# Banded attention with global tokens and a squared-ReLU MLP on one core: global value products in other slots, output copies at the top of a slot, global softmax behind the activation, weight decoding later

## The chip, the cores and the metric

The kernel runs on one core of one Trainium2 chip. The metric is the device time of one execution in microseconds (us), lower is better. Durations come from one profiled execution, the times from unprofiled runs.

## What is computed

Eight batches of eight heads, 512 local tokens, 32 global tokens, head size 64. A local query sees the keys within 32 positions and all global keys; a global query sees every key. The result, 4608 rows of 512, goes through an MLP with 2048 hidden units, squared ReLU, no bias. Everything is float32.

```python
k_all = np.concatenate([k_g, k_l], axis=2); v_all = np.concatenate([v_g, v_l], axis=2)
out_g = np.matmul(sm(scale * np.matmul(q_g, k_all.transpose(0, 1, 3, 2))), v_all)
s_ll = np.where(np.abs(pos[:, None] - pos[None, :]) <= 32, scale * np.matmul(q_l, k_l.transpose(0, 1, 3, 2)), -1e9)
s_lg = scale * np.matmul(q_l, k_g.transpose(0, 1, 3, 2))
out_l = np.matmul(sm(np.concatenate([s_lg, s_ll], axis=-1)), np.concatenate([v_g, v_l], axis=2))
x = np.concatenate([out_g, out_l], axis=2).transpose(0, 2, 1, 3).reshape(B * S, H * D)
h = np.maximum(x @ w_in, 0.0)
out = h * h @ w_out
```

Here `sm` is the softmax over the last axis.

## The kernel before

The local work is cut into 128 units t: eight heads for each half (256 queries) of each batch. Eight units make 256 rows of x, which are one MLP block; 16 local blocks and one block of all 256 global rows make 17. A block takes eight MLP steps, each with 256 of the 2048 hidden units.

One loop over slots t = 0 to 145 writes the whole program. Slot t does, for attention, the transposes of unit t-1's probabilities (`transposes`, copied out by `pt_evac` into pts), the scores and softmax of unit t+1 (`begin`, `rise`; ACT takes the exponential, `softmax3` the division a slot later), and in odd slots the value products of the pair t-3, t-2 into one PSUM tile, xa (`av`); `x_evac` then splits xa into a rounded part x_h (ACT) and the rest x_l (DVE). For the MLP it does step m = t-9: `gemm1` (x times w_in into h), `act1` (ReLU on ACT into r, the square r on DVE), `gemm2` of step m-1 (into the two tiles of o), `act2` (the split of r into gh on ACT and gl on DVE). Products of split operands take three matmuls. Blocks start where m % 8 is 0, slots 17, 25, 33 and so on. At m % 8 == 1 `evac` copies the finished block's o into ot on ACT and sends it out; the new block's first `gemm2` writes the same o.

The 32 global rows run along: each unit's scores hold its global queries' scores too, collected in sg (`g_copy`, `g_add`). After every four units of a batch's second half, so twice in 16 slots, a chain of jobs follows, put on a list by slot and place: `g_soft` (DVE maximum), `g_exp` (ACT exponential), `g_norm` (two small DVE steps), `g_load_v` (gv), `g_tr` (transposes), `g_evac` (copies into gp), `g_av` (ten value products, in the other half of xa), `g_xs` (ACT, xa into gxs) and `g_x` (eight 32x32 DVE transposes into xg). For the second batch these lists start at units 27 and 31, and so on every 16 slots.

The weights come as 64-bit numbers in 32 chunks: a load (`w_load`, into wr), a conversion on ACT (`w_abs`, into wf) and two DVE steps (`w_bits`, the letter "b" in the table `PLAN`). From block 1 on split weights are used: `w_split` (letter "s") makes ws, one ACT and one DVE step. `PLAN` has a row for each slot from 0 and four places in it: behind the softmax, ahead of `act1`, behind `act2` and at the end. `w_need` does ahead of its place what a step needs at once. `LOOK` is how many chunks ahead of the decoding loads are issued, as far as buffers are free (32 in all). Units below 16 use unsplit float32 operands, as does block 0.

TensorE's instructions keep the written order throughout; VectorE's and ScalarE's from slot 17 on (`FREE`), before that a scheduler orders them. All loads and stores are on one queue, SP's. On each engine an instruction that waits holds those behind it. All compute instructions are recorded by one helper, line 53, so the profile is read by tile names.

Of the kernel before, what the change touches and what calls it, by code (L numbers as in the profile page):

```python
# [7 lines left out]
F32 = mybir.dt.float32  # L8
# [8 lines left out]
P = 128  # L17
# [8 lines left out]
NSTEP = NBLK * 8  # L26
# [2 lines left out]
SCALE = 0.125  # L29
CHUNKS = ((0, 128), (320, 128), (128, 96), (224, 96))  # L30

PLAN = [",,,b", "b,,,b", "b,,,b", "b,,b,", "b,,b,", "b,,b,", "b,,b,", "b,b,,b", "b,b,,b", "bb,bb,bb,bb", "bb,bb,bb,bb", "bbs,bb,bbs,bbs", "bbs,bbs,bbs,bbs", "bbs,bbs,bbs,bbs", "bbs,bbs,bs,s", "ss,s,s,s", "ss,s,s,s", "s,,s,", "s,,s,", "s,,s,", "s,,s,", "s,,s,", "s,,s,"]
FREE = (17, 17, 0)
LOOK = 2
SQ = (0, 8)
WCH = 32

# [1 line left out]
def f(ap):  # L39
    return ap.bitcast(F32)  # L40
# [19 lines left out]
def attention_moe(  # L60
# [10 lines left out]
    nc = tc.nc  # L71
# [4 lines left out]
    p2 = ctx.enter_context(tc.tile_pool(name="p2", bufs=2))  # L76
# [15 lines left out]
    def w_take(n):  # L92
        w_bufs["free"] -= n

    def load_head(t):
        raw = pq.tile([P, QK], F32, tag="raw", name=f"raw{t}")
        v = pv.tile([P, VC], F32, tag="v", name=f"v{t}")
        nc.sync.dma_start(raw, qk[t])
        nc.sync.dma_start(v, vv[t])
        heads[t] = dict(raw=raw, v=v)  # L100

    load_head(0)
    con = cp.tile([P, P + 4 * WIN], F32, name="con")
    for o, e in ((0, P + 2 * WIN), (P + 2 * WIN, P + 4 * WIN)):
        nc.sync.dma_start(con[:, o:e], consts[:, o:e])
# [154 lines left out]
    def x_evac(t):  # L260
        g, c = t // 8, (t % 8) // 2
        x = xa[:, :HALF]
        if g == 0:
            ac.copy(xg[:, c, :], x)
        else:
            ac.copy(x_h[:, g % 2, c, :], x)
            ve.tensor_sub(x_l[:, g % 2, c, :], x, f(x_h[:, g % 2, c, :]))
        heads[t] = heads[t + 1] = None

    state = {}  # L270

    def g_load(t):

        b, grp = t // 16, (t // 4) % 2
        qr = p2.tile([P, P], F32, tag="qr", name=f"qr{t}")
        nc.sync.dma_start(qr, qg[b, grp])
        state["q", t // 4] = qr

    def g_split(t):
        if plain(t):  # L280
# [144 lines left out]
    def act2(m):  # L425
        r = moe["r"]
        if m < 8:
            moe["g", m] = (r,)
            return
        gh = p2.tile([P, 2, HALF], F32R, tag="gh", name=f"gh{m}")  # L430
        gl = p2.tile([P, 2, HALF], F32R, tag="gl", name=f"gl{m}")
        ac.copy(gh, r)
        ve.tensor_sub(gl, r, f(gh))
        moe["g", m] = (gh, gl)
# [23 lines left out]
    def evac(blk, tiles=(0, 1)):  # L458
        for i in tiles:
            ot = p2.tile([P, DM], F32, tag="ot", name=f"ot{blk}_{i}")  # L460
            ac.copy(ot, moe["o"][i])
            if blk < NGR:
                b, hf = divmod(blk, 2)
                r0 = b * 544 + 32 + hf * 256 + i * P
                nc.sync.dma_start(out[r0 : r0 + P, :], ot)
            else:
                for bb in range(4):
                    r0 = (4 * i + bb) * 544
                    nc.sync.dma_start(out[r0 : r0 + 32, :], ot[32 * bb : 32 * bb + 32, :])
# [4 lines left out]
    def w_start(i):  # L474
        while w_next["load"] < min(WCH, i + LOOK) and w_bufs["free"] >= 2:
            w_take(1)
            w_load(w_next["load"])
            w_next["load"] += 1
        if i < w_next["load"] and i not in w_ready and (i % 2 == 1 or w_bufs["free"] >= 1):
            w_ready.add(i)  # L480
            w_abs(i)
# [29 lines left out]
    def w_tick(t, place):  # L511
        if t < len(PLAN):
            for c in PLAN[t].split(",")[place]:
                {"b": w_pass, "s": w_chunk}[c]()
# [19 lines left out]
    def run_jobs(t, place):  # L534
        for job, *args in jobs.pop((t, place), ()):
            job(*args)

    def begin(t):
        scores(t)
        g_scores(t)  # L540

    def rise(t):
        softmax1(t)
        softmax2(t)

    g_load(0)
    w_start(0)
    begin(0)
    rise(0)
# [2 lines left out]
    for t in range(NSTEP + LAG + 1):  # L552
        m = t - LAG
        ve.on, ac.on, pe.on = [t >= x for x in FREE]
        prev, run, live, more = 1 <= t <= NT, 0 <= m < NSTEP, t < NT, t + 1 < NT
        pair = t - 3 if t % 2 and 3 <= t <= NT + 1 else None
        if t + 4 < NT:
            load_head(t + 4)
        if t % 4 == 0 and t + 4 < NT:
            g_load(t + 4)  # L560
        if run:
            w_need(m)

        if pair is not None:
            av(pair)
            x_evac(pair)
        run_jobs(t, "av")
        run_jobs(t, "tr")
        if prev:
            transposes(t - 1)  # L570
        if more:
            begin(t + 1)
        if run:
            gemm1(m, 0)
            gemm1(m, 1)
        if prev:
            pt_evac(t - 1)
        run_jobs(t, "evac")
        if live:
            softmax3(t)  # L580
        if t + 2 < NT:
            split_head(t + 2)
        if more:
            rise(t + 1)
        if 0 < m <= NSTEP and m % 8 == 1 and m > 8:
            evac(m // 8 - 1)
        w_tick(t, 0)
        if more:
            g_copy(t + 1)
            g_add(t + 1)  # L590
        run_jobs(t, "soft")
        if t % 4 == 2 and t + 2 < NT:
            g_split(t + 2)
        w_tick(t, 1)
        if run:
            act1(m)
        run_jobs(t, "late")
        if live and t % 4 == 3 and (t // 8) % 2 == 1:
            d = t if t % 8 == 3 else t + 1
            e = d + 4 if d % 2 else d + 5  # L600
            for at, place, job in (
                (d + 1, "soft", g_soft),
                (d + 1, "soft", g_exp),
                (d + 2, "soft", g_norm),
                (d + 2, "late", g_load_v),
                (d + 3, "tr", g_tr),
                (d + 3, "evac", g_evac),
                (e, "av", g_av),
                (e, "evac", g_xs),
                (max(e, 17), "late", g_x),  # L610
            ):
                jobs.setdefault((at, place), []).append((job, t))
        if m == NSTEP:
            for i in range(2):
                gemm2(m - 1, 0, (i,))
                gemm2(m - 1, 1, (i,))
                evac(NBLK - 1, (i,))
        elif m > 0:
            gemm2(m - 1, 0)
            gemm2(m - 1, 1)  # L620
        if run:
            act2(m)
        w_tick(t, 2)
        if 0 < m <= 8:
            w_done(m - 1)
        w_tick(t, 3)
        if 8 * NGR - 2 <= m < 8 * NGR:
            cols = (slice(0, 224), slice(224, HALF))[m % 2]
            ac.copy(x_h[:, 0, :, cols], xg[:, :, cols])
            ve.tensor_sub(x_l[:, 0, :, cols], xg[:, :, cols], f(x_h[:, 0, :, cols]))  # L630
# [69 lines left out]
```

## Time and profile before

| | |
|---|---|
| median of 3 runs | 1136.09 us (1134.98 to 1137.07) |
| profiled execution | 1137.75 us, its span 1135.9 |
| PE, DVE, ACT busy in the span | 1052.2, 669.6, 552.6 us |
| mean granted clock | 0.972 |
| HBM read, written | 65.54 MB, 8.91 MB |

A row of the timeline has the start, the time until the end, engine, line, operation, tiles written and read, shape and count; in square brackets the engine's idle time before it and who ended that. A row of the waits has the total, the number and the longest. A row by stretch has its limits, its length, then busy time of PE, PEld, DVE, ACT and POOL with instruction counts, the granted clock, the share of the DMA engines that is busy and GB/s. Matmuls overlap, so their durations don't add up; start to start does.

### The profile page before, as it was taken

The numbers are of one execution on the slowest core, as the hardware profiler recorded it, in microseconds if no ns is written. First come the engines' busy times: TensorE is split into PE (matmuls) and PEld (weight loads), VectorE is DVE, ScalarE is ACT, GpSimd is POOL, SyncE is SP. The second block draws the span as 40 slices with busy tenths as digits, with TensorE's granted clock in tenths as the row PEclk, the third lists the DMA queues.
The fourth block names the chain that finished last, engine by engine and source line by source line (L and its number), as shares of the span: only waits on it lengthen the run. The fifth ranks groups of instructions, "written<-read, shape, count | busy, mean of one in ns | idle before, by whom it ended". The sixth has DMA issues, their size and how long they took to land.

```text
span 1135.9 us, 21870 instructions
## 1 busy us (share of the span) xinstructions
PE 1052.2 (93%) x8320; PEld 878.9 (77%) x8320; DVE 669.6 (59%) x2340; ACT 552.6 (49%) x1617; POOL 0.5 (0%) x5
## 2 busy tenths in 40 slices
PE   5898799998999989998999989998999989999998
PEld 4665578877888778877888778877888778878987
DVE  5886466565666556655666656656566666663321
ACT  5786445545554445544455454545454454543222
POOL 0000000000000000000000000000000000000000
PEclk9798989999999999999999999999999999999999
DMA  8881111121211212121211212112211212101000
GB/s 267 275 298 52 32 58 48 52 62 57 61 56 40 62 53 62 59 59 48 66 42 53 62 52 62 58 53 61 57 45 56 58 53 66 43 1 43 1 20 19
DMA packets 72458, 75.88 MB, mean 67 GB/s; under 512 B 6304, under 2 KB 63776, under 8 KB 72352
## 3 DMA queue, kind: packets, MB, share of 16 engines
q1 hardware_dynamic: 72352, 74.47, 21.6%
q8 instruction: 66, 1.08, 0.4%
q14 instruction: 40, 0.33, 0.1%
HBM read 65.54 MB, written 8.91 MB: 66 GB/s over the span
## 4 chain that ended last, share of the span: by engine, by line
PE 53%; DVE 23%; ACT 14%; issue 4%; DMA 4%; SPq 0%; ACTq 0%; DVEq 0%
PE o L53 22%; PE h L53 19%; PE xa L53 6%; DVE prob L53 6%; ACT prob L53 5%; PE sb L53 3%; DVE gl L53 3%; DVE r L53 3%; ACT gh L53 2%; PE pt L53 2%; DVE st L53 2%; DVE lo L53 2%; ACT r L53 2%; ACT sg L53 2%; DMA wr<-in_w_dram 2%
## 5 line engine op out<-in xcount | busy, mean ns | idle before, releaser
L53 PE MATMUL h<-x_h,ws 128*128 128x256 f32 x2048 | 400.8, 289 | 6.1 <-DVE r L53 6.1
L53 PE MATMUL o<-ws,gh 128*128 128x512 f32 x1024 | 326.2, 400 | 25.7 <-ACT ot L53 25.7
L53 PEld LDWEIGHTS h<-x_h,ws 128*128 128x128 f32 x2048 | 327.6, 191 | 22.0 <-DVE r L53 7.5
L53 PE MATMUL h<-x_l,ws 128*128 128x256 f32 x1024 | 289.9, 283 | 0.1
L53 ACT ACTIVATE prob<-prob,st 128x224 f32<-128x224 f32 x256 | 121.3, 475 | 259.9 <-DVE st L53 259.7
L53 PEld LDWEIGHTS o<-ws,gh 128*128 128x128 f32 x1024 | 187.0, 192 | 62.2 <-ACT ot L53 29.3
L53 PE MATMUL o<-ws,gl 128*128 128x512 f32 x512 | 203.5, 398 | 0.0
L53 PEld LDWEIGHTS h<-x_l,ws 128*128 128x128 f32 x1024 | 196.1, 192 | 1.0 <-DVE x_l L53 0.4
L53 DVE TENSOR_TENSOR sg<-sb,sg 32x128 f32<-32x128 f32 (+3 forms) x280 | 60.1, 257 | 159.5 <-ACT sg L53 159.3
L53 DVE TENSOR_TENSOR r<-h,r 128x512 f32<-128x512 f32 x128 | 88.4, 691 | 104.2 <-ACT r L53 104.0
L53 DVE TENSOR_TENSOR gl<-r,gh 128x512 fp32r<-128x512 f32 x128 | 88.7, 693 | 77.3 <-ACT gh L53 76.8
L53 ACT CAST gh<-r 128x512 fp32r<-128x512 f32 x128 | 79.3, 619 | 97.5 <-DVE r L53 97.5
L53 PEld LDWEIGHTS o<-ws,gl 128*128 128x128 f32 x512 | 97.7, 191 | 22.9
L53 ACT ACTIVATE r<-h 128x512 f32<-128x512 f32 x136 | 81.3, 598 | 61.1 <-PE h L53 58.1
L53 DVE CUSTOM_DVE_ANT_0 prob<-sb,con 128x224 f32<-128x224 f32 x248 | 86.4, 386 | 9.4 <-PE sb L53 9.1
L53 DVE COPY pts<-pt 128x256 f32<-128x256 f32 x128 | 53.5, 418 | 40.5 <-PE pt L53 40.0
L53 DVE TENSOR_SCALAR prob<-prob,st 128x224 f32<-128x224 f32 x256 | 74.7, 334 | 4.2
L53 ACT COPY pts<-pt 128x256 f32<-128x256 f32 x128 | 47.5, 371 | 60.0 <-PE pt L53 59.0
L53 PEld LDWEIGHTS xa<-pts,v 128*64 128x64 f32 (+1 forms) x768 | 47.5, 141 | 35.8 <-issue 24.1
L53 PEld LDWEIGHTS pt<-con,prob 64*128 64x128 f32 (+1 forms) x1024 | 42.3, 137 | 41.5 <-issue 27.5
L53 PE MATMUL xa<-pts,v 128*64 128x128 f32 (+1 forms) x768 | 73.9, 327 | 0.2 <-ACT pts L53 0.2
L53 PE MATMUL pt<-con,prob 64*128 64x64 f32 (+1 forms) x1024 | 61.7, 242 | 8.0 <-DVE prob L53 7.9
(69 smaller groups left out, 1050.4 us busy)
## 6 DMA issues: line engine op xcount, KB each, us to landing
raw<-in_qk_dram SPq DMA_DIRECT2D x128, 176.0 KB, 2.3
wr<-in_w_dram SPq DMA_DIRECT2D x32, 512.0 KB, 5.5
v<-in_vv_dram SPq DMA_DIRECT2D x128, 96.0 KB, 1.9
gv<-in_vg_dram SPq DMA_DIRECT2D x32, 320.0 KB, 3.4
out_dram<-ot SPq DMA_DIRECT2D x32, 256.0 KB, 2.0
qr<-in_qg_dram SPq DMA_DIRECT2D x32, 64.0 KB, 2.3
out_dram<-ot SPq DMA_DIRECT2D x8, 64.0 KB, 1.7
con<-in_consts_dram SPq DMA_DIRECT2D x1, 288.0 KB, 4.3
```

The source lines that it names most:

```text
L53: r = method(*args, **kwargs)
```

## The change

Five things move; the instructions are the same ones, in the same numbers, on every engine.

- `evac` goes from behind `rise` to the top of the slot, ahead of everything that ACT does in it.
- `g_av` and `g_xs` go from odd slots (where `av` runs) to even ones: one slot later for one of the two chains, one earlier for the other.
- `g_soft`, `g_exp`, `g_norm` and `g_x` go to a new place, "post", behind `act2`; they were ahead of `act1`, `g_x` between `act1` and `act2`.
- `PLAN` does fewer decode steps in slots 0 to 8 and fewer splits before slot 17; `LOOK` goes from 2 to 4.
- the first global queries (qr of `g_load(0)`) are loaded behind unit 0's inputs, not behind the masks and units 1 to 3.

```diff
-PLAN = [",,,b", "b,,,b", "b,,,b", "b,,b,", "b,,b,", "b,,b,", "b,,b,", "b,b,,b", "b,b,,b", "bb,bb,bb,bb", ...]
+PLAN = [",,,b", ",,,b", ",,,b", ",,,b", ",,,b", ",,,b", ",,,b", ",,,b", "b,b,b,b", "b,bb,bbb,bb", ...]
-LOOK = 2
+LOOK = 4
...
     load_head(0)
+    g_load(0)
...
-    g_load(0)
     w_start(0)
...
+        if m > 8 and m % 8 == 1:
+            evac(m // 8 - 1)
         if pair is not None:
             av(pair)
             x_evac(pair)
...
-        if 0 < m <= NSTEP and m % 8 == 1 and m > 8:
-            evac(m // 8 - 1)
         w_tick(t, 0)
...
-            e = d + 4 if d % 2 else d + 5
+            e = d + 5 if d % 2 else d + 4
             for at, place, job in (
-                (d + 1, "soft", g_soft),
-                (d + 1, "soft", g_exp),
-                (d + 2, "soft", g_norm),
+                (d + 1, "post", g_soft),
+                (d + 1, "post", g_exp),
+                (d + 2, "post", g_norm),
                 (d + 2, "late", g_load_v),
                 (d + 3, "tr", g_tr),
                 (d + 3, "evac", g_evac),
                 (e, "av", g_av),
                 (e, "evac", g_xs),
-                (max(e, 17), "late", g_x),
+                (max(e, 17), "post", g_x),
...
             act2(m)
+        run_jobs(t, "post")
         w_tick(t, 2)
```

ScalarE around slots 33 and 34, first before, then changed (gst31: the global exponential; r24, gh24: step 24; ot2: block 2's output; pts33, hi36: unit 33's transposed probabilities, unit 36's rounded inputs):

```order
L53 ACTIVATE sg_107,gst31_2864<-sg_107,gst31_2864 128x544
L53 ACTIVATE r24_2868<-h24_2818 128x512
L53 CAST gh24_2883<-r24_2868 128x512
L53 COPY pts33_2934<-pt0_112 128x4x64
L53 CAST hi36_2941<-raw36_2699 128x352
L53 ACTIVATE prob1_109,st35_2945<-prob1_109,st35_2945 128x224 x2
L53 COPY ot2_0_2951<-o0_2_2165 128x512
L53 COPY ot2_1_2954<-o1_2_2166 128x512
```

```order
L53 ACTIVATE r24_2864<-h24_2818 128x512
L53 CAST gh24_2879<-r24_2864 128x512
L53 ACTIVATE sg_109,gst31_2883<-sg_109,gst31_2883 128x544
L53 COPY ot2_0_2891<-o0_2_2165 128x512
L53 COPY ot2_1_2894<-o1_2_2166 128x512
L53 COPY pts33_2940<-pt0_114 128x4x64
L53 CAST hi36_2947<-raw36_2679 128x352
L53 ACTIVATE prob1_111,st35_2951<-prob1_111,st35_2951 128x224 x2
```

The global exponential has moved from ahead of r24 to behind gh24, and the two output copies from behind the softmax exponentials to right behind it, ahead of pts33 and hi36.

TensorE at the global value products of the chain of unit 27, before (slot 31) and changed (slot 32):

```order
L53 MATMUL xa_114<-pts29_2534,v29_1987 64x128
L53 MATMUL xa_114<-pts28_2430,v28_1896 64x128
L53 MATMUL xa_114<-pts29_2534,v29_1987 64x128
L53 MATMUL xa_114<-gv27_2458,gp27_2537 64x128 x10
L53 MATMUL pt0_112<-con_89,prob0_108 128x64
```

```order
L53 MATMUL o0_2_2165<-ws23_1477,gl21_2581 128x512
L53 MATMUL o1_2_2166<-ws23_1477,gh21_2580 128x512 x2
L53 MATMUL o1_2_2166<-ws23_1477,gl21_2581 128x512
L53 MATMUL xa_116<-gv27_2456,gp27_2537 64x128 x10
L53 MATMUL pt0_114<-con_91,prob1_111 128x64
```

They stood behind the pair 28, 29's local value products in the same tile; now they stand behind a w_out product, in a slot without local ones.

VectorE at `g_x` of the same chain, before (slot 31) and changed (slots 32 and 33):

```order
L53 TENSOR_TENSOR r22_2672<-h22_2624,r22_2672 128x512
L53 STREAM_TRANSPOSE xg_106<-gxs27_2652 32x32 x8
L53 TENSOR_TENSOR gl22_2696<-r22_2672,gh22_2695 128x512
L53 COPY pts31_2748<-pt1_113 128x4x64
L53 TENSOR_SCALAR st32_2662<-st32_2662 128x2
```

```order
L53 TENSOR_TENSOR r23_2761<-h23_2713,r23_2761 128x512
L53 TENSOR_TENSOR gl23_2777<-r23_2761,gh23_2776 128x512
L53 STREAM_TRANSPOSE xg_108<-gxs27_2741 32x32 x8
L53 TENSOR_TENSOR x_l_107<-xa_116,x_h_106 128x256
L53 COPY pts32_2843<-pt1_115 128x4x64
```

The eight transposes have moved from between r and gl to behind gl, ahead of the next slot's x_l.

More of the change, by code (lines that the diff above doesn't have):

```diff
@@ L30 @@
 CHUNKS = ((0, 128), (320, 128), (128, 96), (224, 96))
-PLAN = [",,,b", "b,,,b", "b,,,b", "b,,b,", "b,,b,", "b,,b,", "b,,b,", "b,b,,b", "b,b,,b", "bb,bb,bb,bb", "bb,bb,bb,bb", "bbs,bb,bbs,bbs", "bbs,bbs,bbs,bbs", "bbs,bbs,bbs,bbs", "bbs,bbs,bs,s", "ss,s,s,s", "ss,s,s,s", "s,,s,", "s,,s,", "s,,s,", "s,,s,", "s,,s,", "s,,s,"]
+PLAN = [",,,b", ",,,b", ",,,b", ",,,b", ",,,b", ",,,b", ",,,b", ",,,b", "b,b,b,b", "b,bb,bbb,bb", "b,bb,bbb,bb", "b,bb,bbbs,bbs", "b,bb,bbbs,bbs", "bs,bb,bbbs,bbs", "bs,bb,bbbs,bbs", "b,bb,bbss,bs", "s,s,s,", "s,,s,s", "s,,s,s", "s,,s,", "s,,s,", "s,,s,", "s,,s,", "s,,s,"]
 FREE = (17, 17, 0)
-LOOK = 2
+LOOK = 4
 SQ = (0, 8)
@@ L100, in load_head, with g_load @@
         heads[t] = dict(raw=raw, v=v)
+    state = {}
+    def g_load(t):
+        b, grp = t // 16, (t // 4) % 2
+        qr = p2.tile([P, P], F32, tag="qr", name=f"qr{t}")
+        nc.sync.dma_start(qr, qg[b, grp])
+        state["q", t // 4] = qr
     load_head(0)
+    g_load(0)
     con = cp.tile([P, P + 4 * WIN], F32, name="con")
@@ L268, in x_evac @@
         heads[t] = heads[t + 1] = None
[L270 to L277, printed above, removed]
     def g_split(t):
```

## The prediction, made before the changed kernel ran

> **What bounds the kernel now.** I read the page's first part, then PE's waits, the busy time by stretch, and the rows of one repeated piece in order of time.
>
> ```profile
> span 1135.9 us, 21870 instructions
> PE 1052.2 (93%) x8320; PEld 878.9 (77%) x8320; DVE 669.6 (59%) x2340; ACT 552.6 (49%) x1617; POOL 0.5 (0%) x5
> ...
> PE xa L53 <- DVE x_l L53: 28.6, 15, 5.4
> PE o L53 <- ACT ot L53: 25.7, 15, 3.8
> ...
> PE h L53 <- DVE r L53: 6.1, 7, 1.1
> PE sb L53 <- DMA qr<-in_qg_dram: 4.6, 1, 4.6
> ```
>
> PE is busy in 93% of the span, so of the 1135.9 us only 84 are idle. PE's own waits name 60.4 of them: 28.6 in which the global value products (into xa) wait for DVE's x_l, 25.7 in which a block's first w_out product (into o) waits for ACT's output copies ot, and 6.1 in which a w_in product (into h) waits for DVE's square r. The 4.6 for qr comes once, at the start.
>
> From slot 26 on the program repeats every 16 slots. The busy time of early stretches, of six such pieces together, of one of them, and of 3.4 us around one wait; then PE's rows from the one piece:
>
> ```profile
> 28.40:56.80 28.40, 23.68 (x150) 17.74 (x151) 23.53 (x88) 20.24 (x65) 0.00 (x0) 0.76 0.82 275
> 88.80:106.36 17.56, 12.12 (x77) 8.57 (x75) 13.69 (x34) 12.32 (x32) 0.00 (x0) 0.81 0.10 26
> 106.36:114.37 8.01, 8.01 (x44) 5.29 (x42) 2.94 (x13) 3.63 (x10) 0.00 (x0) 1.00 0.37 107
> 123.39:204.12 80.73, 72.50 (x562) 59.27 (x561) 49.80 (x174) 39.07 (x114) 0.00 (x0) 0.92 0.17 50
> 204.12:980.80 776.68, 732.49 (x6123) 621.22 (x6121) 476.99 (x1730) 383.24 (x1165) 0.00 (x0) 0.98 0.19 56
> 333.11:462.00 128.89, 121.51 (x1023) 103.14 (x1021) 79.50 (x289) 63.87 (x195) 0.00 (x0) 0.99 0.20 56
> 372.70:376.10 3.40, 3.04 (x30) 2.71 (x32) 0.31 (x1) 0.00 (x0) 0.00 (x0) 0.50 0.02 5
> ...
> 373.06 2.40 PE L53 MATMUL xa<-gv,gp 128*64 128x128 f32 x20 [2.28 <-DVE x_l L53]
> 424.06 1.31 PE L53 MATMUL xa<-gv,gp 128*64 128x128 f32 x20 [0.95 <-DVE x_l L53]
> 438.78 1.09 PE L53 MATMUL xa<-pts,v 96*64 96x256 f32 x12
> 453.31 1.09 PE L53 MATMUL xa<-pts,v 96*64 96x256 f32 x12
> ...
> 398.79 0.39 PE L53 MATMUL h<-x_h,ws 128*128 128x256 f32 x1 [0.84 <-DVE r L53]
> 404.19 0.73 PE L53 MATMUL o<-ws,gh 128*128 128x512 f32 x2 [2.28 <-ACT ot L53]
> ```
>
> Six pieces take 776.68, one 129.4 on the mean; in the one of 128.89 DVE is busy for 79.5 and ACT for 63.9. Such a piece has PE waits of 2.28 and 0.95 (xa), of 2.28 and, in another slot, about 1.0 (ot), and of 0.84 (r): 7.4. In the 3.4 us at a 2.28 us wait the granted clock is 0.50, which costs 1.7 more; over six pieces it is 0.98, so 2% or some 14 us, eight such windows. What PE needs without waits: a slot with and a slot without local value products take 14.53 together (438.78 to 453.31), eight pairs 116.2; with two global value products at 1.31 and two sets of global transposes at about 0.36 (an estimate: eight matmuls of 64 columns) it is 119.6.
>
> **The second limit is the round of ACT and DVE.** Both run in written order from slot 17 on, and a slot's work goes to and fro between them. Rows of slots 48 to 53, where a tile's name tells the step:
>
> ```profile
> 386.49 0.48 ACT L53 ACTIVATE prob<-prob,st 128x224 f32<-128x224 f32 x1 [2.81 <-DVE st L53]
> 390.03 0.69 DVE L53 TENSOR_TENSOR gl<-r,gh 128x512 fp32r<-128x512 f32 x1 [0.69 <-ACT gh L53]
> 390.76 0.42 DVE L53 TENSOR_TENSOR x_l<-xa,x_h 128x256 fp32r<-128x256 f32 x1
> 393.71 0.48 ACT L53 ACTIVATE prob<-prob,st 128x224 f32<-128x224 f32 x1 [2.25 <-DVE st L53]
> 395.60 0.72 DVE L53 TENSOR_REDUCE gst<-sg 128x1 f32<-128x544 f32 x1
> 396.55 0.75 ACT L53 ACTIVATE sg<-sg,gst 128x544 f32<-128x544 f32 x1 [1.33 <-DVE gst L53]
> 397.41 0.60 ACT L53 ACTIVATE r<-h 128x512 f32<-128x512 f32 x1
> 399.30 0.36 ACT L53 COPY pts<-pt 128x256 f32<-128x256 f32 x1
> 399.42 0.69 DVE L53 TENSOR_TENSOR gl<-r,gh 128x512 fp32r<-128x512 f32 x1 [0.69 <-ACT gh L53]
> 399.56 0.49 ACT L53 CAST hi<-raw 128x352 fp32r<-128x352 f32 x1
> 400.03 0.42 DVE L53 COPY pts<-pt 128x256 f32<-128x256 f32 x1
> 401.26 0.52 DVE L53 TENSOR_TENSOR lo<-raw,hi 128x352 fp32r<-128x352 f32 x1
> 402.64 0.48 ACT L53 ACTIVATE prob<-prob,st 128x224 f32<-128x224 f32 x1 [2.59 <-DVE st L53]
> 403.58 1.05 ACT L53 COPY ot<-o 128x512 f32<-128x512 f32 x2
> 409.42 0.41 DVE L53 COPY gp<-pt 128x256 f32<-128x256 f32 x1
> 431.21 1.71 DVE L53 STREAM_TRANSPOSE xg<-gxs 32x32 f32<-32x32 f32 x8
> ```
>
> From start to start: exponential to gl 3.54 us (386.49 to 390.03), gl to the next DVE copy 0.61 (399.42 to 400.03), copy to exponential 2.61 (to 402.64); in a slot with local value products x_l to exponential 2.95 (390.76 to 393.71). So one slot's round is 2.61 + 3.54 + 0.61 = 6.76, the other's 7.10, together 13.86 against PE's 14.53. The round may lag by some 1.3 us before PE waits: the two xa waits differ by 2.28 - 0.95 = 1.33, the lag that the earlier slot has already, and the softmax of slot 49, which puts r off by 2.2 (next part), costs PE 0.84, so 1.36 less.
>
> **The change part by part.** *Global value products in even slots.* They no longer stand behind the x_l of their own slot; the last one ended in the slot before. The 28.6 us go, the 1.31 us of matmuls stay. Their ACT copy (xs) now stands between pts and hi, where ACT has room: hi ends at 400.05 and DVE uses it from 401.26. It costs nothing; without that room it would cost its 0.4.
>
> *Output copies at the top.* ACT is done with gh when PE ends the old block, so the two copies (1.05 us) run while PE has transposes, scores and a w_in product (3 us from 398.79) ahead of the product that needs them. For the round: behind gh come 1.05 of copies, 0.26 of pts and 0.49 of hi; lo waits for hi, but also for gl, a copy and 1.23 us of small steps (400.03 to 401.26), which end no sooner. So in slot 42 the wait goes at no price; in slot 50 the softmax now stands ahead of the copies.
>
> *Global softmax behind act2.* Before, reduce to exponential (0.95) and the exponential (0.86, 396.55 to 397.41) and ACT's wait put r off by 2.2. Now both stand behind gl. In slot 50 ACT then runs exponential, copies, pts and hi before DVE has its lo: 0.61 + 0.95 + 0.86 + 1.07 + 0.26 + 0.49 + 0.04 = 4.28 from gl's start, against 0.61 + 1.23 = 1.84: the round is 2.4 later. In slot 45 x_h waits for the exponential and x_l for x_h: 2.2 later. The 6.1 us of waits for r end there, but the lag is only moved to the slot after.
>
> *g_x, g_norm.* The eight 32x32 transposes (1.71 us, 1.74 with the gap) stood between r and gl, where DVE waits 0.7 for ACT anyway; now all of it stands behind gl; in slot 48 it is ahead of the x_l that slot 49's own w_in product needs. Twice 1.74. g_norm, two tiny instructions: twice about 0.35.
>
> The round over 16 slots is then 8 x 13.86 = 110.9, plus 2.4 + 2.2 (softmax), 3.5 (g_x), 0.7 (g_norm), 1.3 (four qz steps, some 0.3 each, as before) and 1.0 (gp, 0.41 and a shorter one, twice, as before): 122.0. PE needs 119.6, so the round bounds, and PE waits 2.4 in small pieces in slots 45 to 54, where the extra work is. I take 122.1: no lower than 119.6, where PE binds; no higher than 126, if the lag of each of the four heavy slots reached PE but for its 1.3. No wait is over 1 us, so I expect no half clock. Gain 129.4 - 122.1 = 7.3, six pieces: **-44**. Behind them one copy wait of 1.0, one xa wait of 1.5 and 0.4 in the last blocks: **-2.9**.
>
> *Weight decoding later.* Of 64 decode steps the table does 19 before the first w_in product, now 12. The splits into ws: 25 were done before slot 17, now 16.
>
> ```profile
> DVE x_l L53 <- ACT x_h L53: 28.1, 32, 7.0
> ACT wf L53 <- DMA wr<-in_w_dram: 16.8, 4, 10.1
> L53 DVE SCALAR_TENSOR_TENSOR wf<-wr,wf 128x512 int32<-128x512 int32 x32 | 22.1, 690 | 0.3
> L53 DVE TENSOR_TENSOR ws<-wf,ws 128x512 fp32r<-128x512 f32 x32 | 21.5, 689 | 9.7 <-ACT ws L53 9.6
> L53 ACT CAST ws<-wf 128x512 fp32r<-128x512 f32 x32 | 18.9, 615 | 0.0
> ```
>
> Slots 14 to 15 took 17.56 us and the next 8.01: ACT had a stack of splits ahead of x_h, x_l waited 7.0 for it, and PE's xa for x_l. With half the stack and xa elsewhere I count 9.5: **-8.1**. Seven decode steps fewer, 0.69 and a shorter one in turn, some 0.56 of DVE: **-3.9**. qr third in the queue instead of twelfth: at most -4.6, but ACT's first weight waits for its DMA for 10.1 us as before, so **-1.3**. Against it: 16.8 MB of weights and 6 MB of other input at 275 GB/s take some 84 us, and work that is 5 us earlier meets weights that are not: **+3.5**, between 0 and +8.
>
> Slots 17 to 25 carry 16 splits instead of 7. Each puts the round off by about 0.6 (0.62 of ACT ahead of r, or 0.69 of DVE behind gl): 14 of them 8.5; the softmax of slot 17 with g_x and two splits ahead of the copies 2.4 + 1.74 + 1.1 = 5.3; another g_x, g_norm and gp 2.6: 16.4 in four pairs of slots. These have 4 x 0.67 + 1.7 (global PE work) of slack and 1.3 of lag, so PE waits 10.7, with some 3 of half clock. Before, this stretch took 80.73 where PE needs 67.6: 13.1 lost. So **+1**, between -5 and +8.
>
> One rule speaks against counting the clock. The Trainium skill, "TensorE: Matmul & The Clock Gate", Part 1, lets the clock fall to half after an idle window of about 3.4 us; by it a wait of 2.28 us would not do that, and the windows would have another cause. The row above has 0.50 right at such a wait; what is left if the windows stay is the third rival.
>
> Sum: -44 - 2.9 - 8.1 - 3.9 - 1.3 + 3.5 + 1 = **-55.7**. The profiled execution took 1137.75 (span 1135.9 and 1.85 around it), 1.7 above the median of the runs, 1136.09. Against the median that is **1080**.
>
> **Rivals.** (1) *PE alone bounds*, because more of the round overlaps than I add. For: PE shows no wait in 12 of a piece's 16 slots. Against: the 0.84 and the 1.33 are what the round gives. Six pieces lose 15 more, slots 17 to 25 some 10: 1055.
> (2) *The weights decide the first 125 us*: they reach ACT late, and 16 splits hold slots 17 to 23 longer. For: 275 GB/s with DMA engines 82% busy. Against: ACT waited for weights 4 times in all. The start's gain (9.8) goes and 8 come on top: 1098.
> (3) *The half clock is not due to the waits* and stays: 14 us, 1094. Against: none is needed to explain the waits, and 0.50 stands at 2.28.
> (4) *Slower*: the softmax behind gl holds ACT's queue, so pts, hi and the scores two slots on come late, and PE waits there. My count is 2.3 per softmax; the change breaks even at about 6.9 (a piece of 131.4, since the rest gains 11.7). At 7.5: 1143.
> (5) *xa waits all the same*, now for the xs of the slot before: the 28.6 stay, 1109. Against: xs is queued right behind pts, early in its slot.
>
> **How the numbers follow.** Forecast 1080, chance 0.58, alone 1068 to 1092. Rivals: (1) 0.16, (2) 0.11, (3) 0.08, (4) 0.04, (5) 0.03. The range 1056 to 1101 reaches into (1) to (3) and leaves out half of (1), (4) and (5). A measurement of this kernel tells about 0.2% from no change: faster by more 0.95, within 0.01, slower 0.04.
>
> **What would show it.** Right: no PE wait for ot over 1 us behind slot 25, none for x_l at the global products; new waits of 0.5 to 0.9 of h for DVE r in slots 51 and 53 and their like; clock 1.00 in the pieces, 122 each; slots 15 to 16 in 10 us; the first w_in product some 4 us earlier; slots 17 to 25 in 78 to 86. Wrong: pieces of 119.6 or of over 125; the first 123.4 us no shorter; PE waiting for pts, hi or the scores' inputs.

## The result, and the profile after

The changed kernel takes 1073.32 us (median of 4 runs, 1071.90 to 1074.31), the kernel before 1136.58 on the same chip: a ratio of 0.9441 with a 95% interval of 0.9421 to 0.9462, 63 us less. The forecast was 1080, and 1068 to 1092 for itself alone.

The page's first part, the granted clock and transfer rate in 40 slices of the span, and the chain that ended last:

```profile
span 1070.7 us, 21923 instructions
PE 1038.6 (97%) x8320; PEld 868.7 (81%) x8320; DVE 665.9 (62%) x2340; ACT 545.4 (51%) x1617; POOL 0.5 (0%) x5
...
PEclk9899899999999999999999999999999999999999
...
GB/s 266 300 331 50 51 55 42 62 61 58 66 65 36 63 83 46 58 63 62 66 58 38 69 74 46 66 44 74 66 62 39 69 73 46 39 1 45 1 21 21
...
DVE 38%; PE 28%; ACT 24%; issue 7%; DMA 1%; SPq 0%; ACTq 0%
```

The same two rows, transfer rate and chain, of the kernel before:

```profile
GB/s 267 275 298 52 32 58 48 52 62 57 61 56 40 62 53 62 59 59 48 66 42 53 62 52 62 58 53 61 57 45 56 58 53 66 43 1 43 1 20 19
...
PE 53%; DVE 23%; ACT 14%; issue 4%; DMA 4%; SPq 0%; ACTq 0%; DVEq 0%
```

PE is busy for 97% of the span, and only 32 us are idle. No slice from the sixth on has a clock digit under 9. The chain has changed its owner: before, 53% of it was PE's, 23% DVE's and 14% ACT's; now DVE has 38% and ACT 24%, PE 28%.

The table of waits (total, times, longest), PE's own and ACT's for weights:

```profile
PE pt L53 <- DVE prob L53: 11.0, 3, 7.4
...
PE o L53 <- ACT ot L53: 5.0, 8, 2.0
...
PE h L53 <- DVE r L53: 3.1, 12, 0.3
PE sb L53 <- DVE sg L53: 3.0, 2, 2.9
...
ACT wf L53 <- DMA wr<-in_w_dram: 2.6, 1, 2.6
```

The same stretches as before (time, then busy us of PE, PE's weight loads, DVE, ACT and POOL, then the granted clock, the DMA share and GB/s):

```profile
82.75:91.77 9.02, 9.02 (x57) 5.97 (x55) 8.10 (x24) 7.54 (x21) 0.00 (x0) 1.00 0.09 22
91.77:101.00 9.23, 9.23 (x64) 6.32 (x62) 3.24 (x15) 4.03 (x11) 0.00 (x0) 1.00 0.16 41
110.02:189.82 79.80, 73.10 (x563) 59.73 (x561) 54.62 (x182) 42.00 (x121) 0.00 (x0) 0.94 0.18 51
189.82:918.89 729.07, 723.81 (x6123) 613.27 (x6121) 474.28 (x1729) 377.91 (x1167) 0.00 (x0) 1.00 0.21 60
918.89:1070.70 151.81, 146.49 (x1038) 128.61 (x1036) 57.25 (x157) 48.97 (x117) 0.00 (x0) 0.99 0.06 20
```

The wait for x_l (28.6 before) is gone altogether, the wait for ot fell from 25.7 to 5.0, and 3.7 of what is left stands in slot 18 (1.95 and 1.74). ACT waits 2.6 for weights instead of 16.8. Slots 17 to 26 still have half clock: from 123.68 to 130.51 us, at the two waits in slot 18, and from 157.81 to 161.23, at PE's wait of 2.88 for sg. Against the stretches before:

| stretch | before, us | after, us | difference | predicted |
|---|---|---|---|---|
| up to the first w_in product of slot 14 | 88.80 | 82.75 | -6.05 | -1.7 |
| slot 14 to 17 | 34.59 | 27.27 | -7.3 | -8.1 |
| slot 17 to 26 | 80.73 | 79.80 | -0.9 | +1 |
| six pieces of 16 slots | 776.68 | 729.07 | -47.6 | -44 |
| from slot 122 on | 155.15 | 151.86 | -3.3 | -2.9 |
| span | 1135.9 | 1070.7 | -65.2 | -55.7 |

A piece takes 121.5 us on the mean; 129.4 before, 122.1 predicted.

Where the rest of a piece's waits comes from, in slots 49 to 51, and last the scores of slots 52 and 53: rows of DVE, ACT and PE in order of time (start, us, engine, what is done, and in brackets the wait ahead of it):

```profile
372.26 0.69 DVE L53 TENSOR_TENSOR gl<-r,gh 128x512 fp32r<-128x512 f32 x1 [0.69 <-ACT gh L53]
...
372.87 0.71 DVE L53 TENSOR_REDUCE gst<-sg 128x1 f32<-128x544 f32 x1
...
373.80 0.75 ACT L53 ACTIVATE sg<-sg,gst 128x544 f32<-128x544 f32 x1 [1.57 <-DVE gst L53]
...
374.41 0.58 DVE L53 TENSOR_SCALAR prob<-prob,st 128x224 f32<-128x224 f32 x2
...
374.55 1.05 ACT L53 COPY ot<-o 128x512 f32<-128x512 f32 x2
...
375.17 0.73 PE L53 MATMUL o<-ws,gh 128*128 128x512 f32 x2 [0.21 <-ACT ot L53]
...
375.75 0.50 ACT L53 CAST hi<-raw 128x352 fp32r<-128x352 f32 x1
...
376.29 0.53 DVE L53 TENSOR_TENSOR lo<-raw,hi 128x352 fp32r<-128x352 f32 x1 [1.30 <-ACT hi L53]
...
380.90 0.39 PE L53 MATMUL h<-x_h,ws 128*128 128x256 f32 x1 [0.27 <-DVE r L53]
...
396.02 0.35 PE L53 MATMUL sb<-hi 64*128 64x224 f32 x2
...
403.05 0.60 PE L53 MATMUL sb<-hi 64*128 64x224 f32 x2
403.05 0.41 PEld L53 LDWEIGHTS sb<-hi 64*128 64x128 f32 x2 [0.24 <-DVE sg L53]
```

From gl's start to lo's start it is 376.29 - 372.26 = 4.03 us; the prediction had 4.28 here. DVE has its small steps done at 374.99 and waits 1.30 for hi, which stands behind the global exponential and the two ot copies on ACT. PE feels little of it: 0.21 at the product that needs ot, 0.27 at the w_in product that needs r. No gap between PE's matmuls in the six pieces is over 0.28. Of the 2.2 us that a piece has above PE's need (119.3, below) 0.88 is idle time of PE ((729.07 - 723.81) / 6); the other 1.3 stands in PE rows that last longer (723.81 us busy, against 715.80 for the same matmuls in a run below), such as the scores of slot 53 (the last rows above): there a weight load waits 0.24 for sg, and the two matmuls that took 0.35 a slot earlier are recorded with 0.60. By slots the loss is narrow. Against the kernel below in whose pieces PE never waits, 13 of the slots 42 to 57 take the same time to 0.01 us; slots 49, 50 and 53 take 6.98, 9.09 and 7.60 us instead of 6.76, 8.08 and 6.76.

### The profile page after: what moved, and what is told of

It reads as the page before. It is cut to its first block, busy times and chain, and to the rows that moved or that the text cites. A ratio compares the mean times of both kernels' runs of the same rounds, so it can differ in the third digit from the quotient of the medians.

```text
span 1070.7 us, 21923 instructions
## 1 busy us (share of the span) xinstructions
PE 1038.6 (97%) x8320; PEld 868.7 (81%) x8320; DVE 665.9 (62%) x2340; ACT 545.4 (51%) x1617; POOL 0.5 (0%) x5
## 2 busy tenths in 40 slices
DMA packets 72458, 75.88 MB, mean 71 GB/s; under 512 B 6304, under 2 KB 63776, under 8 KB 72352
## 4 chain that ended last, share of the span: by engine, by line
DVE 38%; PE 28%; ACT 24%; issue 7%; DMA 1%; SPq 0%; ACTq 0%
PE h L53 12%; PE o L53 11%; DVE prob L53 8%; ACT prob L53 7%; DVE r L53 6%; DVE gl L53 6%; ACT gh L53 5%; ACT r L53 5%; ACT sg L53 4%; DVE st L53 4%; DVE lo L53 4%; DVE pts L53 3%; PE xa L53 2%; DVE xg L53 2%; PE sb L53 2%
## 5 line engine op out<-in xcount | busy, mean ns | idle before, releaser
L53 PE MATMUL o<-ws,gh 128*128 128x512 f32 x1024 | 321.3, 394 | 5.0 <-ACT ot L53 5.0
L53 PEld LDWEIGHTS o<-ws,gh 128*128 128x128 f32 x1024 | 184.3, 189 | 39.3 <-ACT ot L53 6.8
L53 DVE TENSOR_TENSOR lo<-raw,hi 128x352 fp32r<-128x352 f32 x112 | 58.1, 519 | 9.6 <-ACT hi L53 9.6
L53 ACT COPY sg<-sb 32x128 f32<-32x128 f32 (+3 forms) x312 | 57.8, 238 | 11.2 <-DVE st L53 8.1
```

The source lines that it names most:

```text
L53: r = method(*args, **kwargs)
```

## The experiments

The times of the stretches are from one profiled execution each, cut at the first w_in product of slots 17, 26 and 122. Ratios are against runs of the kernel before on the same chip, with 95% intervals; that kernel's median there lay between 1135.18 and 1137.69. The mean granted clock moves between executions of one kernel (in the changed one 0.990 with 1071.90 us, 0.983 with 1074.31), so differences of 2 or 3 us between single profiles are weak.

| kernel | median, us | ratio | to slot 17 | 17 to 26 | one piece | slot 122 on |
|---|---|---|---|---|---|---|
| before | 1136.58 | 1 | 123.39 | 80.73 | 129.45 | 155.15 |
| changed | 1073.32 | 0.9441 (0.9421 to 0.9462) | 110.02 | 79.80 | 121.51 | 151.86 |
| value products alone | 1100.50 | 0.9682 (0.9657 to 0.9708) | 114.94 | 75.93 | 125.79 | 153.26 |
| output copies alone | 1103.63 | 0.9711 (0.9683 to 0.9739) | 122.62 | 75.88 | 124.75 | 153.84 |
| softmax behind act2 alone | 1141.83 | 1.0041 (1.0020 to 1.0062) | 122.42 | 81.22 | 130.10 | 155.74 |
| decoding table alone | 1131.14 | 0.9950 (0.9930 to 0.9970) | 109.31 | 82.20 | 129.94 | 154.90 |
| changed, softmax part undone | 1065.24 | 0.9387 (0.9371 to 0.9402) | 109.51 | 77.36 | 120.77 | 152.00 |
| changed, transposes twice | 1109.47 | 0.9773 (0.9758 to 0.9787) | 111.54 | 84.29 | 126.34 | 153.85 |
| changed, old decoding table | 1067.98 | 0.9412 (0.9392 to 0.9432) | 112.11 | 76.84 | 121.44 | 151.86 |
| changed, extra work hidden | 1053.29 | 0.9271 (0.9252 to 0.9290) | 110.06 | 74.57 | 119.30 | 151.84 |
| changed, transposes hidden | 1058.17 | 0.9320 (0.9303 to 0.9337) | 110.25 | 76.12 | 119.42 | 151.90 |
| hidden, splits early | 1053.67 | 0.9284 (0.9261 to 0.9307) | 111.73 | 73.00 | 119.30 | 151.90 |
| hidden, splits early, gp late | 1053.35 | 0.9282 (0.9265 to 0.9300) | 110.64 | 72.55 | 119.30 | 151.91 |

### One part of the change at a time

**The value products alone.** On the kernel before:

```diff
-            e = d + 4 if d % 2 else d + 5
+            e = d + 5 if d % 2 else d + 4
```

> The kernel before with one part of the change: the global value products in even slots. The theory has it that each wait of TensorE is a loss of its own: the 28.6 us of waits of xa for x_l go, and with them about half of the 14 us of half clock (those windows that stood behind xa waits), while the 25.7 us of waits of o for ot and the 6.1 us of h for r stay; some 3 us come back as a longer wait for ot, since the round of ACT and DVE keeps its lag. About 1136.6 - 28.6 - 7 + 3 = 1104 us. The rival (one round sets the pace, and a wait taken away only moves to the next one) expects that the waits for ot and r grow by most of what goes: 1118 us or more. If the half clock had nothing to do with waits, all eight windows stay: 1111 us.

PE's waits:

```profile
PE o L53 <- ACT ot L53: 25.7, 15, 3.8
...
PE h L53 <- DVE r L53: 8.4, 7, 1.2
```

1100.5, a little better than the 1104 of the theory. The wait for x_l is gone, the wait for ot is 25.7 as it was, to a tenth, and only the wait for r took something back (6.1 to 8.4). The waits are losses of their own; the rival that they move to the next one falls.

**The output copies alone.**

```diff
+        if m > 8 and m % 8 == 1:
+            evac(m // 8 - 1)
         if pair is not None:
...
-        if 0 < m <= NSTEP and m % 8 == 1 and m > 8:
-            evac(m // 8 - 1)
```

> The kernel before with one part of the change: a block's two output copies at the top of a slot. The theory (each wait is a loss of its own) expects that most of the 25.7 us of waits of o for ot go and the other half of the half clock with them, while the 28.6 us of xa stay: about 1136.6 - 25 - 7 = 1104 us. The rival (a wait taken away moves to the next one) expects longer waits of xa for x_l: 1118 us or more.

PE's waits:

```profile
PE xa L53 <- DVE x_l L53: 30.4, 15, 6.0
...
PE o L53 <- ACT ot L53: 1.0, 1, 1.0
```

1103.6, as the theory said: 25.7 of waits for ot become 1.0, and the 28.6 for x_l stay, at 30.4.

**The softmax, norm and transposes behind act2, alone.**

```diff
-                (d + 1, "soft", g_soft),
-                (d + 1, "soft", g_exp),
-                (d + 2, "soft", g_norm),
+                (d + 1, "post", g_soft),
+                (d + 1, "post", g_exp),
+                (d + 2, "post", g_norm),
...
-                (max(e, 17), "late", g_x),
+                (max(e, 17), "post", g_x),
...
             act2(m)
+        run_jobs(t, "post")
```

> The kernel before with one part of the change: the global softmax, its norm and the eight small transposes behind the MLP activation. The theory (the lag is only moved to the slot after, where x_h and the output copies stand) expects no gain: the 6.1 us of waits of h for r go, the waits for ot get longer by as much or more, 1136 to 1142 us. The rival (the waits for r are a loss of their own) expects 1130 us.

PE's waits:

```profile
PE o L53 <- ACT ot L53: 35.4, 15, 5.7
PE xa L53 <- DVE x_l L53: 29.4, 15, 4.8
```

1141.8, slower by 0.4% and at the upper end of the theory's range. No wait for r is left; the wait for ot grew by 9.7. The lag is moved to the slot after, as the prediction said, and it costs more there than what was saved.

**The decoding table alone** (the table PLAN as in the change, LOOK 4, the first global queries loaded right behind the first head).

> The kernel before with one part of the change: weight decoding by the later table, four weights looked ahead instead of two, the first global queries loaded earlier. The theory expects that the first w_in product of slot 14 is 6 us earlier, as in the changed kernel, and that slots 15 and 16, where xa still stands behind x_l, lose part of their 9: some 3 to 5 us less; slots 17 to 25, with 16 splits instead of 7 and all old waits, 0 to 4 us more. From slot 26 on nothing changes. 1136.6 - 6 - 4 + 2 = 1129 us, between 1124 and 1133. The rival (the weights decide) expects that slots 17 to 25 give it all back: 1136 us or more.

1131.1. Slot 17 begins 14.1 us earlier (123.39 to 109.31), and slots 17 to 26 lose 1.5. (In this profiled execution the pieces took 129.94, 0.5 more than before, though nothing differs in them; six of them are 3 us.) The four parts alone make -37.2, -34.1, +4.1 and -6.6 against the 1137.69 of their kernel before, -73.7 together; the whole change makes -63.3. The stretches say where most of the difference goes. The stretch from slot 14 to 17 is counted twice: the value products alone bring slots 14 to 17 from 34.59 to 27.26, the table alone to 28.73, both together 27.27. And slots 17 to 26 gain 4.8 by the products alone and 4.9 by the copies alone, but 0.9 by everything: with the waits gone, the splits and the softmax that were put there set the pace, and there is the half clock named above.

### Is it the round, or PE?

**The softmax part undone in the changed kernel** (the four job places of the diff above back to what they were).

> The changed kernel with the global softmax, its norm and the eight small transposes back in their old places (softmax and norm ahead of r, transposes between r and gl). The theory (the round of ACT and DVE bounds the pieces) counts for a piece: softmax 2.2 per set as before, since it now puts r off instead of what follows gl; the transposes 1.05 instead of 1.74, because DVE waits 0.69 there for ACT's gh; the norm nothing instead of 0.35. That is 2 x 1.05 = 2.1 less in the round, of which PE can take what it waits now beyond the wait of 1.2 for r that comes back (seen where only the value products are moved): 0.1 to 0.6 per piece less, 1069 to 1073 us. Rival one (the parts add up as they were measured alone, +4.7): 1068.6 us. Rival two (r directly ahead of PE's w_in product is the worst place, each of the waits of 6.1 us adds to today's): 1079 us.

PE's wait for r, and the six pieces:

```profile
PE h L53 <- DVE r L53: 9.1, 9, 1.2
```

```profile
186.87:911.49 724.62, 716.80 (x6122) 610.67 (x6121) 474.93 (x1730) 382.47 (x1167) 0.00 (x0) 1.00 0.21 60
```

1065.2: this part of the change costs 0.5% of the time (0.9387 against 0.9441), more than the 0 to 4 us the theory gave it, and below rival one's 1068.6 too. A piece takes 120.77 instead of 121.51, with one wait of 1.19 for r in each, as expected. Another 2.4 come from slots 17 to 26, which none of the three counted; there the clock is at 0.50 in one stretch of 3.4 us here and in three in the changed kernel's profile, so part of it may be the clock.

**The eight small transposes twice.**

```diff
                 (max(e, 17), "post", g_x),
+                (max(e, 17), "post", g_x),
```

> The changed kernel with the eight small transposes of a global head group done twice (the second set writes the same values again, so the result is the same): 1.71 us more of DVE work behind gl, twice in 16 slots. The theory (the round of ACT and DVE bounds a piece now, 121.4 against the 119.3 that PE needs) expects 2.5 to 3.5 us per piece more and the same rate in the slots before and after: 1090 to 1098 us. The rival (PE alone bounds the pieces, the 2 us of small waits have other causes) expects at most 1077 us.

Two of PE's waits, and the six pieces:

```profile
PE sb L53 <- DVE sg L53: 15.9, 8, 3.5
PE h L53 <- DVE x_l L53: 13.8, 7, 2.0
```

```profile
195.83:953.86 758.03, 731.51 (x6122) 620.91 (x6120) 494.84 (x1825) 378.89 (x1165) 0.00 (x0) 0.99 0.20 57
```

1109.5, above the theory's 1098, and 36 us more than the changed kernel for 3.5 us of DVE work in a piece. A piece goes from 121.51 to 126.34, 4.8 more: beyond the 2.5 to 3.5 of the theory, because the new waits (2.0 for x_l, 2.1 for sg) are long enough for half clock again, six stretches in six pieces; at 1.7 each that is 1.7 a piece, and 3.1 is left. That PE alone bounds the changed kernel (1077 at most) falls: it has no room for this work.

**The extra work put where its engine waits.** New job places: "pre" behind split_head (ACT has hi out and waits for st), "mid" behind rise (DVE has the maxima out and waits for ACT).

```diff
             split_head(t + 2)
+        run_jobs(t, "pre")
         if more:
             rise(t + 1)
+        run_jobs(t, "mid")
         w_tick(t, 0)
...
-                (d + 1, "post", g_soft),
-                (d + 1, "post", g_exp),
-                (d + 2, "post", g_norm),
+                (d + 1, "mid", g_soft),
+                (d + 2, "pre", g_exp),
+                (d + 2, "mid", g_norm),
...
-                (max(e, 17), "post", g_x),
+                (max(e, 17), "mid", g_x),
```

> The changed kernel with the global softmax's extra work put where its engine waits anyway: DVE's reduce, norm and small transposes behind the maxima of the scores and ahead of the score adds and r (DVE waits 1.39 for ACT's sg and 0.30 for r there), ACT's global exponential one slot later behind hi and ahead of the local exponential (ACT waits 2.3 to 3.0 for DVE's st there). The theory (the round bounds a piece by what stands in its line) takes 2.4 + 2.2 + 3.5 + 0.7 = 8.8 us out of the round, which is then some 113: PE bounds, a piece takes 119.3 to 120.0, six pieces 8 to 12 us less, slots 17 to 25 some 3 less: 1059 to 1065 us. The rival (PE's small waits have other causes, ot and the gaps ahead of xa and pt) expects 1071 us or more.

Slots 17 to 26, and the six pieces:

```profile
110.06:184.63 74.57, 71.07 (x562) 58.52 (x561) 54.36 (x182) 41.93 (x121) 0.00 (x0) 0.98 0.19 55
184.63:900.43 715.80, 715.80 (x6123) 610.16 (x6121) 477.43 (x1730) 385.24 (x1167) 0.00 (x0) 1.00 0.21 61
```

1053.3, under the theory's 1059. In the six pieces PE is busy for 715.80 of 715.80 us: a piece is 119.30, PE's own work and nothing else. The instructions are those of the changed kernel, only their places differ; so the 2.2 us that a piece of the changed kernel has above 119.3 are the round's. ACT's own waits say the same: in slots 42 to 57 it waits for PE three times in the changed kernel (0.28, 0.22 and 0.67), and 15 times, 10.7 us in all, in this one. This kernel beats both: 1.8% faster than the changed one (0.9271 against 0.9441), 7.3% faster than the one before.

**Only the transposes and the norm there.** The softmax stays at "post".

> The changed kernel with only the eight small transposes and the norm moved to where DVE waits anyway (behind the maxima of the scores, ahead of the score adds and r); the global softmax stays behind the MLP activation. With the softmax hidden too a piece took 119.3, and 121.5 in the changed kernel, so 2.2 are to be shared out. The theory (the round adds up: 4.6 for the softmax twice, 4.2 for transposes and norm; PE takes up 1.3 of lag in each heavy slot) expects that the softmax alone leaves some 1 us of waits per piece in slots 50 and 51: 120.0 to 120.6, six pieces 5 to 9 us less than in the changed kernel, 1062 to 1067 us. Rival one (the transposes are all of it) expects 119.3 per piece and 1058 us; rival two (the softmax is all of it) 121.3 and 1072 us.

The six pieces:

```profile
186.37:902.89 716.52, 716.26 (x6122) 610.39 (x6120) 475.38 (x1730) 381.69 (x1167) 0.00 (x0) 1.00 0.21 61
```

1058.2, a piece 119.42: what rival one expected. With the transposes and the norm out of the way 2.1 of the 2.2 us are gone, and the softmax that stays costs 0.1 on the mean (0.7 in the first piece, nothing in the other five). It still delays lo by its two microseconds (4.04 from gl to lo), but with 4.2 less in the line the round is 122.0 - 4.2 = 117.8, under PE's 119.3, and the two delays fit into the slack and the lag. Shares of a sum that is just above a bound can't be split in proportion, as the expectation did: the first 2.7 taken away give all there is. By the same sum hiding the softmax alone would be enough as well (122.0 - 4.6 = 117.4); that was not run, so the run shows that the transposes and the norm are enough, not that they alone are to blame.

### The weights

**The old decoding table in the changed kernel** (PLAN and LOOK as before; the early load of the first queries stays).

> The changed kernel with the old table of weight decoding and two weights looked ahead; the early load of the first global queries stays. The theory of the sum (the start is worth some 5 us by the table, the splits moved into slots 17 to 25 cost some 4) expects that the first w_in product of slot 14 is 4 to 6 us later, that slot 15 stays near 9 because xa no longer waits there, and that slots 17 to 25 take 76 to 78 instead of 80.6: 1073 to 1077 us. The rival (the table is worth here what it was alone, 0.5%) expects 1079 us.

Slots 17 to 26, and the six pieces:

```profile
112.11:188.95 76.84, 70.75 (x563) 58.27 (x561) 49.97 (x175) 38.88 (x114) 0.00 (x0) 0.98 0.19 53
188.95:917.61 728.66, 723.40 (x6123) 613.00 (x6121) 473.94 (x1729) 376.99 (x1164) 0.00 (x0) 1.00 0.21 60
```

1068.0, below the 1073 to 1077 expected; the rival's 1079 falls. By ratio it is 0.9412 against 0.9441 with the new table, and the intervals overlap, so whether the table costs a little or nothing is not settled. The two halves point opposite ways, each by one profile: slot 17 begins 2.1 us later without it, where the theory had 4 to 6, and slots 17 to 26 take 76.84 instead of 79.80, 3.0 less. Neither is firm. The six other kernels here that are built on the changed one and keep its early table have slot 17 at 109.51 to 111.73, against 112.11 without it. And of the 3.0 us 2.35 are PE rows (73.10 against 70.75 us busy), with the clock at 0.50 in three stretches here and in one there. So the table may take back where its 16 splits went what it gives at the start; the runs don't settle how much. And slot 14 begins at 84.84 here against 88.80 before: by these profiles some 2 to 4 us of the start's gain come from the rest, of which the early load of the queries is the only part that acts ahead of slot 10 (2 to 4, because the three single-part kernels with the old start had slot 14 at 87.1 to 88.1).

**Ten of the 16 splits moved into slots 15 and 16**, where DVE is busy for 3.2 and ACT for 4.0 of 9.2 us (the row of slot 15 in the profile after), on the kernel with the extra work hidden; ACT and DVE in written order from slot 15 on, so that the splits are not pulled ahead of the slot's own work.

```diff
-FREE = (17, 17, 0)
+FREE = (15, 15, 0)
...
-"b,bb,bbss,bs", "s,s,s,", "s,,s,s", "s,,s,s", "s,,s,", "s,,s,", "s,,s,", "s,,s,", "s,,s,"]
+"bs,bs,bbsss,bss", "ss,ss,sss,ss", ",,,", "s,,,", "s,,,", "s,,,", "s,,,", "s,,,", "s,,,"]
```

> The kernel with the softmax's extra work hidden (1053.3 us), with 10 of the 16 splits of slots 17 to 23 moved into slots 15 and 16, where ACT and DVE are busy for only 7.6 and 5.1 of 18.3 us, and ACT and DVE in written order from slot 15 on instead of 17, so that the splits stand behind the slot's own work there. The theory (each split in slots 17 to 23 puts the round off by some 0.6, 16 of them 8.5 as the prediction counted) expects that slots 17 to 25 take 69 to 72 instead of 74.6, that slots 14 to 16 stay at 27.3 and the pieces at 119.3: 1048 to 1051 us. The rival (the stack of splits in slots 14 to 16 holds x_h, pts and the scores, as in the kernel before) expects slots 14 to 16 longer by as much: 1053 us or more.

PE's wait for x_h, and slots 17 to 26:

```profile
PE h L53 <- ACT x_h L53: 1.4, 1, 1.4
```

```profile
111.73:184.73 73.00, 69.39 (x563) 56.68 (x561) 51.76 (x178) 40.32 (x119) 0.00 (x0) 1.00 0.19 56
```

1053.7, no change. Slots 17 to 26 are 1.6 shorter, and slot 17 begins 1.7 later, because slot 9 takes 6.54 instead of 4.74. No split stands that early: the half clock of the start ends at 46.58 us in this profile, 3.7 us into slot 9, and at 41.74, ahead of slot 9, in the profile of the kernel it is built on. Why it ended later is open. The stack at the end of slot 16 does hold x_h: PE waits 1.43 for it and 0.73 for x_l in slot 17, a smaller form of what the rival said. The theory's 1048 to 1051 was not reached.

**The gp copies moved too** (ACT's two behind split_head, DVE's two behind rise).

> The kernel of the run on early splits, with the copies of the global probabilities (gp) moved as well: ACT's two behind hi, DVE's two behind the maxima, so that 0.6 us twice in 16 slots leave the round. The theory (PE alone bounds the pieces at 119.3) expects no difference in the pieces and 0 to 2 us in slots 17 to 25: 1047 to 1051 us. The rival (something of the round is left in the 119.3) expects 0.5 per piece less: 3 us beside that.

1053.4, and a piece 119.30 as before: nothing of the round is left in it. The theory's "no difference in the pieces" holds, its 1047 to 1051 us doesn't.

## Why the prediction was right, point by point

**The bound.** Right, and the best of it: PE's waits were the loss, and the round of ACT and DVE, not PE, sets a piece behind the change. The round was added up as 122.0 and is 121.5; PE's need as 119.6 and is 119.3 (where it is busy for all of it). The place holds too: the loss is in slots 49, 50 and 53, and the prediction had it in slots 45 to 54. That the sum is right to 0.5 us is in part luck: it has no wait for PE in it, and ACT has 1.2 us of them in a piece. The rival that PE alone bounds gave 1055 for that case, and the kernel in which it does takes 1053; it is not the changed kernel.

**Value products, -28.6 us of waits; copies, -25.7.** Right. Each alone takes its wait away, but for 1.0 us of the copies', and the other stays. "No ot wait over 1 us behind slot 25" holds (0.23 is the longest), "none for x_l" too.

**Softmax.** The delay of lo was put at 2.4 and is 2.2 (4.03 instead of 4.28 from gl to lo). Its effect on PE was put at waits of 0.5 to 0.9 of h for r in slots 51 and 53. That is wrong in form: the waits for r are 0.27 at most, and the time is lost in small pieces, for ot and r and in weight loads that wait. That the part brings nothing by itself was right (+4.1 alone, where "the lag is only moved").

**Transposes, 2 x 1.74, and norm, 2 x 0.35.** Right as terms of the round: 1.74 twice more cost 3.1 a piece beside the clock, and the run that hides them loses all but 0.1 of the difference from PE's bound. That these 4.2 us could have stood at a place where DVE waits, the prediction didn't ask.

**Half clock.** Right: 1.00 in the six pieces, where 14 us were lost before. The rival that it stays falls. The reason given, that no wait is over 1 us, was enough; the rule behind it is below.

**Slots 14 to 17, -8.1.** From slot 14 to 15 it is 9.02 (9.5 predicted), but from 15 to 16 it is 9.23 instead of 8.01: the moved value products, 1.31, are in it. The prediction said that these 1.31 stay and left them out of this stretch. -7.3 in sum.

**The start: -3.9 - 1.3 + 3.5 = -1.7 predicted, -6.05 found.** This is the step that was off most, and a sum that ends at the first w_in product misses where the gain is. Two rows of the kernel before, then one of the changed kernel:

```profile
14.68 0.83 PE L53 MATMUL pt<-con,prob 64*128 64x64 f32 x8 [3.58 <-DVE prob L53]
...
48.65 0.67 ACT L53 ACTIVATE wf<-wr 128x512 f32<-128x512 f32 x1 [3.59 <-DMA wr<-in_w_dram]
```

```profile
14.88 0.83 PE L53 MATMUL pt<-con,prob 64*128 64x64 f32 x8 [7.39 <-DVE prob L53]
```

The early queries end PE's wait of 4.58 for qr, but the next wait, for prob, grows from 3.58 to 7.39, and the first transposes begin no earlier (14.88 against 14.68 us); ACT's first weight conversion starts at 12.32 us, as before (12.14). So far the prediction's doubt about the queries was right. The first w_in product begins 2.0 us earlier (45.00 to 42.98), where some 4 were expected. The other 4.0 come in slots 9 and 10, which take 4.74 and 9.19 us instead of 7.38 and 10.58 and for which the prediction named nothing. There, before, ACT waits 3.59 for a weight, PE then waits 0.55 and 0.76 for ACT's sg and 0.40 for its r, and the clock is at 0.50 from 51.83 to 55.24; in the changed kernel none of this is left. So by these profiles the "+3.5" for weights that are not there in time had the wrong sign: the weights were late in the kernel before, and come in time now. It was reckoned with the 275 GB/s of one stretch of the trace before; the second and third slice move 300 and 331 GB/s in the changed kernel, 275 and 298 before. Which of the later table, the four weights looked ahead and the early queries does it no run separates. With the old table, two weights ahead and the early queries ACT waits 5.9 for weights in all, and slots 9 and 10 take 5.55 and 9.20. Rival two, the weights decide, falls with this.

**Slots 17 to 25, +1.** -0.9, inside the -5 to +8. The count behind it, some 0.6 per split, gives too much as far as the profiles show: with 9 splits fewer in this stretch (the old table) it is 3.0 shorter, at most 0.33 a split, and with 10 fewer in the kernel with the extra work hidden 1.6, some 0.16 a split; both have less half clock as well. The softmax part is at most 2.4 of it. PE's need, put at 67.6, was not reached: the fullest clock (1.00, ten splits early) has PE busy for 69.39.

**The sum.** -55.7 predicted, -65.2 of span found: 4.4 from the start, 3.6 from the pieces at 0.6 each, 1.9 from slots 17 to 25, 0.4 from the end, less 0.8 in slots 14 to 16.

## What to carry to other kernels

Where two engines pass work to and fro, add up that round, with every extra step in its line, and compare it with the bound of the engine that you want full; when the round is the longer one, an extra step at its end costs nearly its length (3.1 of 3.5 us with the transposes twice, beside the clock), and nothing at a place where its engine waits for the other, so look for those waits (here 1.39 us of DVE for sg and mostly 2.2 to 3.0 of ACT for st in a slot) before placing it. Measure each part of a change alone and undone: here one of four was a loss inside a gain of 5.6%, and another brought 0.5% alone and nothing that can be told from noise within the whole.

## What the runs showed of the hardware

The prediction tied the half clock to the length of a wait; it hangs on where the wait falls. Every change of the granted clock in the thirteen profiles lies on a grid of 3.413 us, to 0.01. Two waits of the same 2.28 us in the kernel before, at 373.06 and 404.19, and two of 2.1 and 2.0 in the kernel with the transposes twice, at 418.12 and 379.31, in the stretches of that grid:

```profile
369.26:372.67 3.41, 1.53 (x15) 0.77 (x13) 2.23 (x7) 2.15 (x7) 0.00 (x0) 1.00 0.21 56
372.67:376.09 3.42, 3.03 (x30) 2.70 (x32) 0.34 (x2) 0.00 (x0) 0.00 (x0) 0.50 0.02 7
...
399.98:403.40 3.42, 1.93 (x17) 1.73 (x15) 2.52 (x12) 0.83 (x4) 0.00 (x0) 1.00 0.16 41
403.40:406.81 3.41, 2.62 (x11) 2.18 (x12) 1.73 (x6) 2.58 (x9) 0.00 (x0) 1.00 0.45 168
406.81:410.22 3.41, 3.41 (x48) 2.61 (x47) 2.14 (x7) 2.13 (x6) 0.00 (x0) 1.00 0.23 61
```

```profile
377.68:381.10 3.42, 1.78 (x15) 1.79 (x16) 3.19 (x13) 0.00 (x0) 0.00 (x0) 1.00 0.07 19
381.10:384.51 3.41, 3.41 (x26) 2.62 (x26) 1.70 (x8) 2.08 (x7) 0.00 (x0) 1.00 0.20 53
...
415.23:418.65 3.42, 1.32 (x15) 0.79 (x15) 1.71 (x9) 2.08 (x7) 0.00 (x0) 1.00 0.19 55
418.65:422.06 3.41, 3.41 (x22) 3.15 (x18) 2.66 (x8) 1.28 (x3) 0.00 (x0) 0.50 0.02 5
```

The first number behind the length is PE's busy time. The stretch with 1.53 busy (1.88 idle) is followed by one at 0.50; the wait of the same length that is cut by the edge, 1.49 idle in one stretch and 0.79 in the next, leaves 1.00. So in the other kernel: 2.10 idle is followed by 0.50, 1.64 is not. Counted over all thirteen profiles behind the first 50 us, in stretches at full clock: 54 of 54 with PE idle for 1.85 us or more were followed by half clock, 3 of 34 between 1.4 and 1.85, and 1 of 3757 below (1.13 idle). That is a limit at a little over half of the stretch, seen here only and not tried by a run made for it. The Trainium skill, "TensorE: Matmul & The Clock Gate", Part 1, has the free-running window of about 3.4 us, and the grid agrees with it; that a window has to be idle from end to end is how the prediction read it, and the rows contradict that.
